# Attention over a key and value cache, one token: key-value groups taken in pairs

## The chip, the cores and the metric

One core of a Trainium2 chip. The metric is the device time of one execution in microseconds. A core has TensorE (PE), VectorE (DVE), ScalarE (ACT), GpSimd (POOL) and SyncE (SP), which here issues all large loads from device memory (HBM) into on-chip memory (SBUF, 128 partitions); 16 DMA engines carry them. TensorE adds up in PSUM.

## The reference

One new token (a row of 512) goes through an attention block and an MLP block. The attention has 32 query heads, 8 key-value groups of 4 query heads each, a cache of 16384 tokens a group and 128 values a token; all tensors are bf16.

```python
q = (layernorm(x) @ wq).reshape(1, 1, 32, 128)           # wq: 512 x 4096, 4 MB
scores = einsum(q, k) * 128 ** -0.5                      # k_cache: 8 groups x 16384 x 128, 32 MB
o = einsum(softmax(scores), v)                           # v_cache: the same size, 32 MB
h = x + o.reshape(1, 1, 4096) @ wo                       # wo: 4096 x 512, 4 MB
# block B on layernorm(h), S = 1: its four shifted quarters take other tokens, of which there
# are none, so they are zero and x1 is its input
x1 = layernorm(h)
out = h + x1 + gelu(layernorm(x1) @ w3) @ w4             # w3: 512 x 1792, w4: 1792 x 512
```

Each byte of the cache and of the weights is used once: 79 MB are read and 1 KB is written.

## The kernel before

The kernel records operations by engine (class `Program`), with what each reads and writes; `emit` puts them out engine by engine in recorded order and derives the semaphore waits. Nothing is rescheduled, so each engine, SP too, works through its list in order, and one that waits holds back all that stands behind it.

**Buffers.** Four buffers of 32 KB a partition (`rb`, 4 MB each) form a ring. The list `ORDER` deals the large loads out to them in turn: query weights, keys 0, keys 1, then values g and keys g+2 for each group g, at last the output weights and the MLP weights. A load waits until the last reader of its buffer is done: for keys the DVE transpositions, for values the products with them, for the query weights the query products. A fifth buffer of the same size, `kt`, holds the transposed keys in eight slices.

**Queries.** Layer norm on 128 partitions (`row_sums`, `variance`, `seeds`, `inverse_root`) gives `xn`. 128 products (L363) with one moving column make the 32 query heads as columns `QT`; four selecting products (L369) and four copies (L374) spread them into `qb`, in which zeros stand around each query so that a shifted window picks the output rows.

**One group** (loop over g from 0 to 8, in which the values of group g-1 stand between the steps of group g):
- `transpose_keys`: eight DVE transpositions (L384), each of 1024 32-bit words a partition (pairs of bf16), from `rb` to `kt`.
- `scores`: 32 products (L392) of 512 columns into one PSUM bank. 128 output rows are 32 parts of the tokens times 4 heads, 512 columns are the tokens of a part.
- `max_a` (L399) takes the maximum of a row, `max_b` (L403, L405) turns the 128 maxima into a row and takes one for each head, `max_c` (L409, L411) spreads them back as the bias, and ACT makes Exp and its sum (L414). `weights` transposes the result into `pt` (L419), `denominator` adds the sums up (L423).
- `values`: 32 products (L433), four side by side in column groups of the array: 16 stationary columns (4 token rows x 4 heads) against 512 moving columns (4 token rows x 128). Only the blocks in which both token rows agree are wanted.
- `gather`: a copy of the whole bank to SBUF (L441) and four fp32 products (L444) with the selecting matrix `zo`, which pick the wanted blocks and add them up in `A_ps` over all groups.
- then SP gets the loads of values g and keys g+2 (all loads are at L216).

**The end.** `A_ps` is normalised (L487 to L493) to `o_b`; 128 products with the output weights (L499); layer norm; 16 products with w3 (L514); Gelu (L527); transpositions (L531); 56 products with w4 (L538); the sum (L542); the store (L544). `spin` puts idle products on PE in between (L245). The output weights are loaded in two pieces and the MLP weights in six, so that products can begin before all has landed.

Of the kernel before, what the change touches and what calls it, by code (L numbers as in the profile page):

```python
# [109 lines left out]
D = 512  # L110
HQ = 32
# [11 lines left out]
RING = 4  # L123
ORDER = [("wq", 0), ("k", 0), ("k", 1)]
ORDER += [x for g in range(HKV) for x in (("v", g), ("k", g + 2)) if x[1] < HKV] + [("wo", 0), ("ffn", 0)]
SLOT = {x: n % RING for n, x in enumerate(ORDER)}
QB, PB, FB = SLOT["wq", 0], SLOT["wo", 0], SLOT["ffn", 0]
# [7 lines left out]
def bass_sequential_preLN__gqa_block_cached__mixer_s_mlp__decode_kernel(  # L135
# [13 lines left out]
    with ExitStack() as ctx:  # L149
# [12 lines left out]

        x4 = sb("x4", [4, 128], BF16)
# [3 lines left out]
        selq_f = sb("selq_f", [128, 4, 32], FP32)  # L167
        quarter = sb("quarter", [4, 4, 32], BF16)
        selq = sb("selq", [128, 4, 4, 32], BF16)
        row32 = sb("row32", [128, 32], FP32)  # L170
        maskdd = sb("maskdd", [128, 4], FP32)
        zo = sb("zo", [128, 4, 240], FP32)
        zd = sb("zd", [128, 240], FP32)
# [5 lines left out]
        QT = sb("QT", [128, HQ], BF16)  # L179
        qb = sb("qb", [128, 4, HKV, QW], BF16)  # L180
        mx = sb("mx", [128, 1], FP32)
        nm = sb("nm", [128, REP], FP32)
        nmh = sb("nmh", [128, REP], FP32)
        bias = sb("bias", [128, 1], FP32)
        acc = [sb(f"acc{i}", [128, 1], FP32) for i in range(2)]
        p_sb = sb("p_sb", [128, 512], BF16)
        pt = [sb(f"pt{i}", [128, 16, 32], BF16) for i in range(2)]
        o_sb = [sb(f"o_sb{i}", [128, 512], FP32) for i in range(2)]
# [13 lines left out]
        rb = [sb(f"rb{i}", [128, 128 * DH], BF16) for i in range(RING)]  # L202
        kt = sb("kt", [128, 128 * DH], BF16)
        wq_sb, wo_sb = rb[QB], rb[PB]
        w3_sb = rb[FB][:, 0:NCH * FM].rearrange("p (k f) -> p k f", k=NCH)
        w4_sb = rb[FB][:, NCH * FM:2 * NCH * FM].rearrange("p (m c) -> p m c", m=NHC)
# [11 lines left out]
        def load_whole(i, src):  # L218
            load(f"r{i}", rb[i][:, :], src, ("r", i, 0), also=[("r", i, n) for n in range(1, RPARTS)])

        def load_tokens(kind, g):

            src = A_k_cache if kind == "k" else A_v_cache
            load_whole(SLOT[kind, g], src[0, g].rearrange("(p t) d -> p (t d)", p=128))
# [17 lines left out]
        def spin(n):  # L242

            for _ in range(n):
                pe(lambda e: e.matmul(O_ps[1][:, :], pt[0][:, 0:4, :].rearrange("p n u -> p (n u)"), p_sb[:, :],  # L245
                                      start=True, stop=True), r=["p", ("pt", 0)], w=[("O", 1)], bank=[("O", 1)])
# [61 lines left out]
        load_whole(QB, A_wq.rearrange("(p k) c -> p (k c)", k=NCH))  # L308
        load_tokens("k", 0)
        load_tokens("k", 1)  # L310
# [3 lines left out]
        dve(lambda e: e.memset(selq_f[:, :, :], 0.0), w=["selq_f"])  # L314
# [3 lines left out]
        for b in range(2):  # L318
            for e_ in range(2):
                n = 2 * b + e_  # L320
                P.op("POOL", lambda e, n=n, b=b, e_=e_: e.affine_select(
                    out=selq_f[:, n, :], in_=selq_f[:, n, :], pattern=[[-2, 32]], compare_op=ALU.not_equal,
                    fill=1.0, base=-(64 * b + e_), channel_multiplier=1), r=["selq_f"], w=["selq_f"])
# [16 lines left out]
        dve(lambda e: e.tensor_copy(selq[:, :, :, :], selq_f[:, :, :].unsqueeze(2).to_broadcast([128, 4, 4, 32])),  # L340
            r=["selq_f"], w=["selq"])
        dve(lambda e: e.memset(nscale[:, :], -SCALE), w=["nscale"])
        act(lambda e: e.activation(scr[0:1, 0:1], mean4[0:1, 0:1], ACTF.Exp), r=["mean4"], w=["scr"])
        for i in range(2):
            dve(lambda e, i=i: e.memset(O_ps[i][:, :], 0.0), w=[("O", i)], bank=[("O", i)])
        dve(lambda e: e.memset(zo[:, :, :], 0.0), w=["zo"])
        dve(lambda e: e.memset(zd[:, :], 0.0), w=["zd"])
        pool(lambda e: e.memset(qb[:, :, :, :], 0.0), w=["qb"])  # L348
        dve(lambda e: e.tensor_reduce(row32[:, :], ident_f[:, :].rearrange("p (c r) -> p r c", c=4), AX.X, ALU.add),
# [3 lines left out]
        dve(lambda e: e.tensor_copy(  # L353
            zo[:, :, 112:128].rearrange("p j (h d) -> p j h d", d=4),
            row32[:, 0:16].rearrange("p (j h) -> p j h", j=4).unsqueeze(3).to_broadcast([128, 4, 4, 4])),
            r=["row32"], w=["zo"])
        dve(lambda e: e.tensor_copy(zd[:, 112:128].rearrange("p (h d) -> p h d", d=4),
                                    maskdd[:, :].unsqueeze(2).to_broadcast([128, 4, 4])), r=["maskdd"], w=["zd"])


        for h in range(HQ):
            for k in range(NCH):
                pe(lambda e, h=h, k=k: e.matmul(n_ps[:, h:h + 1],  # L363
                                                wq_sb[:, k * HQ * DH + h * DH:k * HQ * DH + (h + 1) * DH],
                                                xn[:, k:k + 1], start=(k == 0), stop=(k == NCH - 1)),
                   r=["xn", ("r", QB, 0)], w=["n"], bank=["mn"])
        dve(lambda e: e.tensor_copy(QT[:, :], n_ps[:, 0:HQ]), r=["n"], w=["QT"], bank=["mn"])
        for n in range(4):
            pe(lambda e, n=n: e.matmul(m_ps[:, n * HQ:(n + 1) * HQ],  # L369
                                       selq[:, n, :, :].rearrange("p a i -> p (a i)"), QT[:, :],  # L370
                                       start=True, stop=True), r=["selq", "QT"], w=["m"], bank=["mn"])
        for a in range(4):
            lo, hi, at = 32 * a, 32 * a + 32, QPAD + 32 * a
            dve(lambda e, lo=lo, hi=hi, at=at: e.tensor_copy(  # L374
                qb[lo:hi, :, :, at:at + REP].rearrange("p n g h -> p (n g) h"),
                m_ps[lo:hi, 0:4 * HQ].rearrange("p (n h) -> p n h", h=REP)), r=["m"], w=["qb"], bank=["mn"])


        def transpose_keys(g, ts):
            i = SLOT["k", g]  # L380
            for t in ts:
                view = lambda x, t=t: x[:, :].bitcast(I32).rearrange("p (x l w) -> p x (l w)", x=2, l=64)[
                    :, :, t * 512:(t + 1) * 512]
                dve(lambda e, i=i, view=view: e.transpose(view(kt), view(rb[i])),  # L384
                    r=[("r", i, n) for n in range(RPARTS)], w=[("kt", t)])
# [3 lines left out]
        def scores(g, cs):  # L389
            for c in cs:  # L390
                for n in range(4):
                    pe(lambda e, g=g, n=n, c=c: e.matmul(  # L392
                        s_ps[:, g % 2, :], qb[:, n, g, QPAD - 4 * c:QW - 4 * c],
                        ktv[:, n // 2, n % 2, :, 8 * c:8 * c + 8, :],
                        start=(c == 0 and n == 0), stop=(c == 7 and n == 3)),
                       r=["qb", ("kt", c)], w=[("s", g % 2)], bank=[("s", g % 2)])

        def max_a(g):
            dve(lambda e, g=g: e.tensor_reduce(mx[:, :], s_ps[:, g % 2, :], AX.X, ALU.max),  # L399
                r=[("s", g % 2)], w=["mx"], bank=[("s", g % 2)])  # L400

        def max_b():
            pe(lambda e: e.matmul(m_ps[0:1, 0:128], mx[:, :], ident_f[:, :], start=True, stop=True),  # L403
               r=["mx", "ident_f"], w=["m"], bank=["mn"])
            dve(lambda e: e.tensor_reduce(nm[0:1, :], m_ps[0:1, 0:128].rearrange("o (n h) -> o h n", h=REP),  # L405
                                          AX.X, ALU.max), r=["m"], w=["nm"], bank=["mn"])

        def max_c(g):
            pe(lambda e: e.matmul(n_ps[:, 0:REP], nscale[0:1, :], nm[0:1, :], start=True, stop=True),  # L409
               r=["nm", "nscale"], w=["n"], bank=["mn"])  # L410
            dve(lambda e: e.scalar_tensor_tensor(nmh[:, :], n_ps[:, 0:REP], 1.0, maskdd[:, :], ALU.mult, ALU.mult,  # L411
                                                 accum_out=bias[:, :]), r=["n", "maskdd"], w=["nmh", "bias"],
                bank=["mn"])
            act(lambda e, g=g: e.activation(p_sb[:, :], s_ps[:, g % 2, :], ACTF.Exp, bias=bias[:, 0:1],  # L414
                                            scale=float(SCALE), accum_out=acc[g % 2][:, :]),
                r=[("s", g % 2), "bias"], w=["p", ("acc", g % 2)], bank=[("s", g % 2)])

        def weights(g):
            dve(lambda e, g=g: e.transpose(pt[g % 2][:, :, :].rearrange("p n u -> p (n u)"), p_sb[:, :]),  # L419
                r=["p"], w=[("pt", g % 2)])  # L420

        def denominator(g):
            pe(lambda e, g=g: e.matmul(A_ps[:, 128:129], zd[:, 112 - 16 * g:240 - 16 * g], acc[g % 2][:, :],  # L423
                                       start=(g == 0), stop=(g == HKV - 1), skip_group_check=True),
               r=[("acc", g % 2), "zd"], w=["A"], bank=["A"])

        def values(g, qs):
            i = SLOT["v", g]
# [20 lines left out]
        for g in range(HKV + 1):  # L449
# [4 lines left out]
            if g:  # L454
                values(g - 1, range(2))
# [122 lines left out]
```

## Time and profile before

| | |
|---|---|
| median of 3 runs | 192.53 us (192.48 to 192.58) |
| the profiled execution | 192.57 us, span 191.0 us |
| granted TensorE clock, mean | 0.865 |
| busy: PE, DVE, ACT, POOL | 125.0, 107.5, 10.1, 8.9 us |
| load queue of SP | 79.17 MB, 97.1% of 16 DMA engines over the span |
| loads on that queue | 25: 17 of 4096 KB, 8 smaller |

The span runs from the first to the last instruction of the core; the time of an execution is 1.57 us longer. A line like `L384 DVE STREAM_TRANSPOSE kt<-rb` gives source line, engine, operation and what it writes and reads. In the timeline, the first column is the start in us and the second how long the row's instructions took together; a bracket at the end gives the idle time of the engine before it and what ended it. The packet records of the trace list, for each piece that a DMA engine moves, its queue, start, duration and size; here a piece is one partition's row of a load.

### The profile page before, as it was taken

The page shows a single profiled execution, that of the slowest core. Times are in us where ns is not written, and L with a number is a line of the kernel's source. Part 1 is how long each engine was busy: PE and PEld are TensorE (multiplying, and loading weights), DVE is VectorE, ACT ScalarE, POOL GpSimd, SP SyncE. Part 2 cuts the span into 40 slices and gives each one's busy share as a digit, 9 for nine tenths or more (in the row PEclk, how much of TensorE's full clock was granted, in tenths as well). Part 3 has the DMA queues.
Part 4 walks back from the last instruction along what each step waited for, and adds up shares of the span by engine and source line. Part 5 has one row for each costly group of instructions (what it writes and reads, how often), then busy time and mean ns, then how long its engine had stood idle before and what let it go on. Part 6 is the DMA issues. An engine that isn't in the chain of part 4 may idle for free.

```text
span 191.0 us, 2257 instructions
## 1 busy us (share of the span) xinstructions
PE 125.0 (65%) x979; PEld 56.4 (30%) x979; DVE 107.5 (56%) x178; ACT 10.1 (5%) x22; POOL 8.9 (5%) x19
## 2 busy tenths in 40 slices
PE   1025079579889825993499539972996199736894
PEld 1025024224332321432133313340333033312632
DVE  5822099399399317932794259435953495303171
ACT  3000000100100100010000100010001000400010
POOL 6400000000000000000000000000000000000042
PEclk9999999859999995899569975995798569988699
DMA  6999999999999999999999999999999999999991
GB/s 227 432 439 436 439 439 434 439 439 432 425 422 419 419 425 432 432 429 439 439 439 439 429 425 432 425 425 419 439 419 436 425 439 439 439 396 407 419 399 74
DMA packets 3624, 79.29 MB, mean 415 GB/s; under 512 B 416, under 2 KB 544, under 8 KB 1056
## 3 DMA queue, kind: packets, MB, share of 16 engines
q1 hardware_dynamic: 3608, 79.17, 97.1%
q8 instruction: 7, 0.11, 0.2%
q14 instruction: 1, 0.01, 0.0%
q10 hardware_dynamic: 8, 0.00, 0.0%
HBM read 79.17 MB, written 0.00 MB: 414 GB/s over the span
## 4 chain that ended last, share of the span: by engine, by line
DMA 70%; DVE 21%; PE 6%; SPq 1%; issue 1%; ACT 0%; ACTq 0%
DMA rb<-in_A_k_cache_dram 56%; DVE kt L384 20%; DMA rb<-in_B_w_dram 14%; PE s_ps L392 5%; SPq L216 1%; ACT p_sb L414 0%; DVE pt L419 0%; DVE mx L399 0%; PE mn_ps L538 0%; PE mn_ps L409 0%; PE mn_ps L403 0%; DVE nm L405 0%; DVE fin L542 0%; DVE nmh L411 0%; SPq L101 0%
## 5 line engine op out<-in xcount | busy, mean ns | idle before, releaser
L392 PE MATMUL s_ps<-kt,qb 128*128 128x512 bf16 x256 | 74.1, 452 | 32.8 <-DVE kt L384 32.2
L384 DVE STREAM_TRANSPOSE kt<-rb 128x1024 int32<-128x1024 int32 x64 | 73.0, 1209 | 28.3 <-DMA rb<-in_A_k_cache_dram 28.3
L392 PEld LDWEIGHTS s_ps<-kt,qb 128*128 128x128 bf16 x256 | 27.0, 111 | 77.4 <-DVE kt L384 41.1
L433 PE MATMUL O_ps<-rb,pt 128*16 128x512 bf16 x256 | 20.6, 410 | 3.2 <-DMA rb<-in_A_v_cache_dram 3.2
L444 PE MATMUL A_ps<-o_sb,zo 128*128 128x128 f32 x64 | 9.7, 297 | 7.4 <-DVE o_sb L441 7.4
L414 ACT ACTIVATE p_sb<-s_ps,bias 128x512 bf16<-128x512 f32 x8 | 5.5, 688 | 155.3 <-DVE nmh L411 155.3
L399 DVE TENSOR_REDUCE mx<-s_ps 128x1 f32<-128x512 f32 x8 | 5.5, 692 | 12.4 <-PE s_ps L392 12.4
L444 PEld LDWEIGHTS A_ps<-o_sb,zo 128*128 128x128 f32 x64 | 8.1, 198 | 8.9 <-DVE o_sb L441 8.9
L419 DVE STREAM_TRANSPOSE pt<-p_sb 128x512 bf16<-128x512 bf16 x8 | 5.7, 711 | 7.3 <-ACT p_sb L414 7.3
L441 DVE COPY o_sb<-O_ps 128x512 f32<-128x512 f32 x8 | 5.3, 657 | 8.0 <-PE O_ps L433 8.0
L363 PE MATMUL mn_ps<-xn,rb 128*128 128x1 bf16 x128 | 3.5, 165 | 9.3 <-DMA rb<-in_A_wq_dram 9.3
L433 PEld LDWEIGHTS O_ps<-rb,pt 128*16 128x16 bf16 x256 | 5.9, 91 | 9.8 <-DMA rb<-in_A_v_cache_dram 4.3
L297 POOL TENSOR_SCALAR st<-st 128x1 f32<-128x1 f32 x1 | 0.3, 265 | 176.0 <-DVE st L282 176.0
L363 PEld LDWEIGHTS mn_ps<-xn,rb 128*128 128x128 bf16 x128 | 3.5, 104 | 9.4 <-issue 9.4
L423 PE MATMUL A_ps<-acc,zd 128*128 128x1 f32 x16 | 3.3, 273 | 2.3 <-ACT p_sb L414 2.3
L403 PE MATMUL mn_ps<-ident_f,mx 128*1 128x128 f32 x16 | 3.0, 271 | 2.5 <-DVE mx L399 2.5
L499 PE MATMUL O_ps<-rb,o_b 128*32 128x128 bf16 x128 | 3.4, 300 | 1.8 <-DMA rb<-in_A_wo_dram 1.8
L245 PE MATMUL O_ps<-p_sb,pt 128*128 128x512 bf16 x17 | 4.5, 381 | 0.0
L405 DVE TENSOR_REDUCE nm<-mn_ps 1x4 f32<-1x128 f32 x8 | 2.2, 278 | 3.8 <-PE mn_ps L403 3.8
L423 PEld LDWEIGHTS A_ps<-acc,zd 128*128 128x128 f32 x16 | 2.6, 203 | 5.9 <-ACT p_sb L414 5.9
L348 POOL MEMSET qb<- 128x4992 bf16 x1 | 4.3, 4258 | 0.0
L499 PEld LDWEIGHTS O_ps<-rb,o_b 128*32 128x32 bf16 x128 | 3.2, 142 | 1.9 <-DVE o_b L493 1.9
(74 smaller groups left out, 42.7 us busy)
## 6 DMA issues: line engine op xcount, KB each, us to landing
rb<-in_A_k_cache_dram SPq DMA_DIRECT2D x8, 4096.0 KB, 29.8
rb<-in_A_v_cache_dram SPq DMA_DIRECT2D x8, 4096.0 KB, 34.5
rb<-in_A_wq_dram SPq DMA_DIRECT2D x1, 4096.0 KB, 12.2
rb<-in_A_wo_dram SPq DMA_DIRECT2D x1, 3072.0 KB, 33.0
rb<-in_B_w_dram SPq DMA_DIRECT2D x1, 1344.0 KB, 23.3
rb<-in_A_wo_dram SPq DMA_DIRECT2D x1, 1024.0 KB, 35.1
rb<-in_B_w_dram SPq DMA_DIRECT2D x1, 768.0 KB, 25.5
rb<-in_B_w_dram SPq DMA_DIRECT2D x1, 512.0 KB, 26.3
```

Of the source, the lines that this page charges most:

```text
L245: pe(lambda e: e.matmul(O_ps[1][:, :], pt[0][:, 0:4, :].rearrange("p n u -> p (n u)"), p_sb[:, :], start=True, stop=True), r=["p", ("pt", ...
L363: pe(lambda e, h=h, k=k: e.matmul(n_ps[:, h:h + 1], wq_sb[:, k * HQ * DH + h * DH:k * HQ * DH + (h + 1) * DH], xn[:, k:k + 1], start=(k == ...
L384: dve(lambda e, i=i, view=view: e.transpose(view(kt), view(rb[i])), r=[("r", i, n) for n in range(RPARTS)], w=[("kt", t)])
L392: pe(lambda e, g=g, n=n, c=c: e.matmul(s_ps[:, g % 2, :], qb[:, n, g, QPAD - 4 * c:QW - 4 * c], ktv[:, n // 2, n % 2, :, 8 * c:8 * c + 8, ...
L399: dve(lambda e, g=g: e.tensor_reduce(mx[:, :], s_ps[:, g % 2, :], AX.X, ALU.max), r=[("s", g % 2)], w=["mx"], bank=[("s", g % 2)])
L414: act(lambda e, g=g: e.activation(p_sb[:, :], s_ps[:, g % 2, :], ACTF.Exp, bias=bias[:, 0:1], scale=float(SCALE), accum_out=acc[g % 2][:, :]),
L419: dve(lambda e, g=g: e.transpose(pt[g % 2][:, :, :].rearrange("p n u -> p (n u)"), p_sb[:, :]), r=["p"], w=[("pt", g % 2)])
L423: pe(lambda e, g=g: e.matmul(A_ps[:, 128:129], zd[:, 112 - 16 * g:240 - 16 * g], acc[g % 2][:, :], start=(g == 0), stop=(g == HKV - 1), sk ...
L433: pe(lambda e, q=q, ct=ct, xl=xl, ch=ch: e.matmul(O_ps[g % 2][32 * ct:32 * ct + 16, :], pt[g % 2][:, xl, 4 * ch:4 * ch + 16], tiles[:, xl ...
L441: dve(lambda e, g=g: e.tensor_copy(o_sb[g % 2][:, :], O_ps[g % 2][:, :]), r=[("O", g % 2)], w=[("osb", g % 2)], bank=[("O", g % 2)])
L444: pe(lambda e, g=g, j=j: e.matmul(A_ps[:, 0:128], zo[:, j, 112 - 16 * g:240 - 16 * g], o_sb[g % 2][:, j * 128:(j + 1) * 128], start=False, ...
L499: pe(lambda e, r_=r_, q=q: e.matmul(O_ps[0][32 * q:32 * q + 32, 0:128], copies(o_b[:, r_:r_ + 1], 32), wo_sb[:, r_ * D + q * 128:r_ * D + ...
```

## The change

Two groups are worked on at once: partitions 0 to 63 hold the first group's tokens and 64 to 127 the second's, each partition 256 tokens (64 KB of keys and 64 KB of values).

- **Buffers and loads.** The ring goes. `vb` (64 KB a partition) takes the values of a pair as one load of 8 MB with rows of 64 KB; `kb[0]` and `kb[1]` (32 KB) take the keys of a pair as two loads, the first and the second half of each row. The values of the last pair come as two loads (rows of 48 and 16 KB). The query weights lie in `vb`, the output weights in `kb[0]`, the MLP weights in `kb[1]`. The order is query weights, keys of pair 0 (two halves), values 0, keys of pair 1, values 1, and so on, then the weights as before. The next keys wait for the transpositions from their own buffer, the next values for all products with the values before.
- **Queries.** 32 products with 512 moving columns, `xn` repeated over 64 stationary columns, put the heads of a pair as rows into four PSUM banks; eight DVE transpositions (`qcol`) and four copies make `qb`. The selecting matrices and their five preparing steps, the 128 narrow products, `QT` and two PSUM clears go.
- **Softmax.** One for a pair: maximum and Exp run over 1024 columns in two banks, with 8 heads in the bias. The weights are transposed in two steps of 64 partitions into `pt`, which is zeroed once and holds the two groups in columns of their own. One `pt`, one `acc`. Values stand after the softmax of their own pair, no longer between the steps of the next group.
- **Values.** 64 products a pair, as before two groups had, with 32 stationary columns instead of 16.
- **Gather.** Instead of copy and four products: four DVE steps multiply each block of 128 columns of the bank with a 0/1 mask of rows (`rowc`) and add them up in `od`; one fp32 product with `zo` puts the sum into `A_ps`.

The diff, cut to its core:

```diff
-RING = 4
-ORDER = [("wq", 0), ("k", 0), ("k", 1)]
-ORDER += [x for g in range(HKV) for x in (("v", g), ("k", g + 2)) if x[1] < HKV] + [("wo", 0), ("ffn", 0)]
+PAIRS = HKV // 2
+V3 = ((0, 3), (3, 4))
...
-        rb = [sb(f"rb{i}", [128, 128 * DH], BF16) for i in range(RING)]
+        kb = [sb(f"kb{i}", [128, 128 * DH], BF16) for i in range(2)]
+        vb = sb("vb", [128, 256 * DH], BF16)
         kt = sb("kt", [128, 128 * DH], BF16)
...
+        def pair_rows(src, j):
+            return src[0, 2 * j:2 * j + 2].rearrange("g (u t) d -> (g u) (t d)", u=64)
+
+        def load_keys(j, y):
+            n = 128 * DH
+            load(f"k{y}", kb[y][:, :], pair_rows(A_k_cache, j)[:, y * n:(y + 1) * n], ("r", y, 0),
+                 also=[("r", y, i) for i in range(1, RPARTS)])
+
+        def load_values(j):
+            src = pair_rows(A_v_cache, j)
+            if j < PAIRS - 1:
+                load("v", vb[:, :], src, ("v", 0), also=[("v", 1)])
+            else:
+                n = 64 * DH
+                for i, (lo, hi) in enumerate(V3):
+                    load(f"v3{i}", vb[:, lo * n:hi * n], src[:, lo * n:hi * n], ("v", i))
...
+        rows = [(O_ps[0][:, :], ("O", 0)), (O_ps[1][:, :], ("O", 1)), (s_ps[:, 0, :], ("s", 0)), (s_ps[:, 1, :], ("s", 1))]
+        for j, (row, key) in enumerate(rows):
             for k in range(NCH):
+                for g in range(2):
+                    at = k * HQ * DH + (2 * j + g) * REP * DH
+                    pe(lambda e, row=row, k=k, g=g, at=at: e.matmul(
+                        row[64 * g:64 * g + 64, :], copies(xn[:, k:k + 1], 64), wq_sb[:, at:at + REP * DH],
+                        start=(k == 0), stop=(k == NCH - 1)), r=["xn", ("v", 0)], w=[key], bank=[key])
+            for b in range(2):
+                dve(lambda e, j=j, b=b, row=row: e.transpose(
+                    qcol[:, j, 2 * REP * b:2 * REP * (b + 1), :].rearrange("p m u -> p (m u)"),
+                    row.rearrange("p (h b i e) -> p b e h i", b=2, i=32, e=2)[:, b, :, :, :]),
+                    r=[key], w=["qcol"], bank=[key])
...
+        def softmax(j):
+            s_all = s_ps[:, :, :].rearrange("p y f -> p (y f)")
+            dve(lambda e: e.tensor_reduce(mx[:, :], s_all, AX.X, ALU.max), r=[("s", 0), ("s", 1)], w=["mx"], **both)
...
+            act(lambda e: e.activation(p_sb[:, :], s_all, ACTF.Exp, bias=bias[:, 0:1], scale=float(SCALE),
+                                       accum_out=acc[:, :]),
+                r=[("s", 0), ("s", 1), "bias"], w=["p", "acc"], **both)
+            for g in range(2):
+                dve(lambda e, g=g: e.transpose(pt[64 * g:64 * g + 64, :, :, g, :], p_sb[64 * g:64 * g + 64, :]),
+                    r=["p"], w=["pt"])
...
+        def values(j):
+            tiles = vb[:, :].rearrange("p (x c l d) -> p x l c d", x=4, c=8, l=8)
+            for q in range(16):
                 for ct in range(4):
+                    xl, ch = 2 * q + ct // 2, ct % 2
+                    parts = [int(xl // 8 >= V3[1][0])] if j == PAIRS - 1 else [0, 1]
                     pe(lambda e, q=q, ct=ct, xl=xl, ch=ch: e.matmul(
+                        O_ps[j % 2][32 * ct:32 * ct + 32, :], pt[:, xl, ch, :, :].rearrange("p g u -> p (g u)"),
+                        tiles[:, xl // 8, xl % 8, 4 * ch:4 * ch + 4, :], start=(q == 0), stop=(q == 15)),
+                       r=[("v", n) for n in parts] + ["pt"], w=[("O", j % 2)], bank=[("O", j % 2)])
+
+        def gather(j):
+            O, key = O_ps[j % 2], ("O", j % 2)
+            for c in range(4):
+                block = O[:, c * 128:(c + 1) * 128]
+                if c == 0:
+                    dve(lambda e, block=block: e.tensor_scalar(od[:, :], block, rowc[:, 0:1], None, ALU.mult),
+                        r=[key, "rowc"], w=["od"], bank=[key])
+                else:
+                    dve(lambda e, block=block, c=c: e.scalar_tensor_tensor(
+                        od[:, :], block, rowc[:, c:c + 1], od[:, :], ALU.mult, ALU.add),
+                        r=[key, "rowc", "od"], w=["od"], bank=[key])
+            pe(lambda e: e.matmul(A_ps[:, 0:128], zo[:, 96 - 32 * j:224 - 32 * j], od[:, :], start=False,
+                                  stop=(j == PAIRS - 1), skip_group_check=True),
+               r=["od", "zo"], w=["A"], bank=["A"])
+
+        load_values(0)
+        for j in range(PAIRS):
+            for y in range(2):
+                transpose_keys(y, range(8))
+                scores(j, y, range(8))
+                if j < PAIRS - 1:
+                    load_keys(j + 1, y)
+            softmax(j)
+            values(j)
+            gather(j)
+            if j < PAIRS - 1:
+                load_values(j + 1)
```

## The prediction

> **What bounds the kernel now.** I read the page first, then the chain in order of time, the timeline of SP's issues, the timeline of the last 27 us, and the packet records of the trace.
>
> The page, sections 1 to 3 (queue lines: packets, MB, share of 16 engines' time):
>
> ```profile
> span 191.0 us, 2257 instructions
> PE 125.0 (65%) x979; PEld 56.4 (30%) x979; DVE 107.5 (56%) x178; ACT 10.1 (5%) x22; POOL 8.9 (5%) x19
> ...
> DMA  6999999999999999999999999999999999999991
> GB/s 227 432 439 436 439 439 434 439 439 432 425 422 419 419 425 432 432 429 439 439 439 439 429 425 432 425 425 419 439 419 436 425 439 439 439 396 407 419 399 74
> ...
> q1 hardware_dynamic: 3608, 79.17, 97.1%
> q8 instruction: 7, 0.11, 0.2%
> ```
>
> No compute engine is over 65%; the load queue is full from the second slice to the last but one. 97.1% of 191.0 us is 185.5 us of transfer that can't be overlapped with itself. The change moves the same bytes, so only three things can move the time: the cost of moving them, a hole in the stream, and the work behind its end.
>
> The chain that ended last, in order of time (start us, us, what):
>
> ```profile
> 121.07 29.50 DMA rb<-in_A_k_cache_dram
> 150.57 0.02 issue
> 150.60 9.14 DVE kt L384 x8
> 159.77 0.03 issue
> ...
> 161.59 26.81 DMA rb<-in_B_w_dram
> 188.40 0.04 issue
> 188.45 0.57 PE mn_ps L538 x16
> 189.02 0.02 issue
> 189.04 0.29 DVE fin L542
> ```
>
> The 20% of DVE in this chain is no limit: the weights issued at 159.8 us, after the last key transposition, wait behind loads that are already queued and land in order. The real end is the last weight piece at 188.40 us; 2.6 us follow it (0.57 product, 0.29 sum, the store and its landing).
>
> SP's issues, in the timeline (start us, us, instruction):
>
> ```profile
> 16.72 0.33 SPq L216 DMA_DIRECT2D rb<-in_A_k_cache_dram  x1
> 33.19 0.33 SPq L216 DMA_DIRECT2D rb<-in_A_v_cache_dram  x1
> 47.66 0.33 SPq L216 DMA_DIRECT2D rb<-in_A_k_cache_dram  x1
> ```
>
> Keys 0 land at 23.97 us (the chain's first transfer ends there), keys 7 at 150.57: thirteen 4 MB loads later, so 9.74 us a load. Each issue comes two or three loads ahead of its turn, and the queue never empties.
>
> **The stream, costed.** In the packet records a row of 32,768 B takes 1216 ns (median of 2176), 24,576 B 915 ns, 8192 B 313 ns. The slope is 0.0367 ns a byte, with 12 ns a packet left over. Value rows of 64 KB in pairs 0 to 2 replace 48 packets on each of the 16 DMA engines by 24, so 24 x 12 ns = 0.29 us is saved. Packets overlap by some 3.5 ns, which makes 0.2 us the lower estimate. If a 64 KB row is still moved as two packets, the saving is nothing. No row shows such a packet; as the fit is straight from 8 to 32 KB I take 0.24. Pair 3's values (48 and 16 KB rows) keep their packet count. Three loads fewer save three completion packets of 9 ns, 0.03 us. Sum: -0.27 us, bounds -0.32 and 0.
>
> Keys become halves of 64 KB rows: still 32 KB a packet, only the pitch in memory doubles. The trace has reads of part of a row: the output weights (24 KB and 8 KB out of 32 KB) run at the fitted line, and so do the MLP weights with 14 KB pitch (10,752 B in 407 ns). I cost it at nothing. The Trainium skill speaks against it here ("DMA: Bandwidth & Descriptors", Latency and other measured facts): copies slow down when the row pitch is a large power of two, from 207 of 214 GB/s at 512 KiB to 103 at 4 MiB. Its smallest pitch is eight times this one; an estimate by its 3% over the 67 MB of keys and values would be +5 us. No run here shows it.
>
> **Holes.** The ring gives way to one value buffer of 64 KB and two key buffers, so each issue has a new condition, and SP waits in program order: a late one holds back all behind it. With 9.74 us a unit, in the new order: first half of keys of pair 0 at 23.97, second 33.7, values 53.2, keys of pair 1 at 62.9 and 72.7, and from there 38.9 us a pair. Worst cases:
> - Values 0 wait for the 32 query products. The query weights are in at 13.04. Products of 512 columns took 0.43 us each at half clock (scores from 25.29 on); all serial that is 13.7 us, so issue by 26.7, needed by 33.7.
> - Keys of pair 1, first half, wait for the first 8 transpositions. DVE first has 8 query transpositions of 256 columns (0.57 each by the 224-column row, mostly beside the products) and four copies of 0.29: free by 29; then 9.14: issue at 38, needed by 53.2. Second half: 48 against 62.9.
> - Values 1 wait for values 0 to be read: softmax done by 57, then 64 products. The last group's 32 took 3.50 us cold, 109 ns each (16 warm took 1.04): 7.0 us, issue at 64, needed by 72.7. This is the thinnest margin, 8.7 us, and it repeats in each pair.
> - Output weights wait for transpositions over at 150, MLP weights for 159.8; their turn is 170.
>
> So no hole, price 0. If the cover goes, each us past 8.7 costs one.
>
> **The tail.** What the one softmax for a pair lengthens shows only after the last keys. These are the rows of before:
>
> ```profile
> 161.34 0.69 DVE L399 TENSOR_REDUCE mx<-s_ps 128x1 f32<-128x512 f32 x1 [1.62 <-PE s_ps L392]
> ...
> 164.33 0.71 DVE L419 STREAM_TRANSPOSE pt<-p_sb 128x512 bf16<-128x512 bf16 x1 [0.91 <-ACT p_sb L414]
> ...
> 170.06 3.50 PE L433 MATMUL O_ps<-rb,pt 128*16 128x512 bf16 x32 [3.22 <-DMA rb<-in_A_v_cache_dram]
> ...
> 177.48 3.36 PE L499 MATMUL O_ps<-rb,o_b 128*32 128x128 bf16 x128 [1.82 <-DMA rb<-in_A_wo_dram]
> ```
>
> Keys still land at 150.57 (fifteenth unit in both orders). From mx to the end of pt took 3.70 us. The maximum doubles its columns (+0.54, 0 to 0.69), Exp too (+0.5, 0 to 0.69), and the weight transposition becomes two of 1024 columns on 64 partitions: by columns 2 x 1.4 = 2.8, by elements 1.4; I take 2.8, so +2.1. pt is ready at 168.2, not 165.0. Then 64 products instead of 32, three quarters of them with values landed at 165.2: 4.2 us warm, 7.0 cold, ending at 172.4 to 175.2 (before: 173.56). The diagonal sums replace a copy (0.69) and 8 products (1.16) by four DVE steps on 128 columns (0.29 to 0.35 each, 1.4) and two passes (0.38): a wash. Normalising follows as before 1.98 and 1.17 us later: o_b at 175.5 to 178.3 against 176.71. It is needed when the first output-weight piece lands (177.48), and behind that the MLP's last products wait 0.29 and 0.30 us for their weights: 0.59 more is free. Cost 0 to 0.2; I take 0.
>
> The query products (128 to 32), the fewer gathers and the removed set-up lie under the loads and count nothing: queries are needed at 23.97, end at the latest at 29, and the 5 us is taken up before the values of pair 0 arrive.
>
> **Sum.** The profiled execution took 192.57 us (191.0 span, 1.57 around it), the median of the runs is 192.53. 192.57 - 0.27 = 192.30; from the median 192.26. I predict 192.3. About 0.2%, 0.39 us, is what a measurement can tell from no change: 192.14 and 192.92 are the limits.
>
> **Rivals.**
> 1. *The last DMA engine ends earlier: faster, 191.9.* The 1 KB packets of the last piece fall in two groups: eight engines are through at 186.1 to 186.7 us, eight at 187.4 to 188.26. There are eight instruction packets inside the span (seven of 16 KB on q8, one of 8 KB on q14), and beside a q8 packet an engine stood still for 1.0 us and its next row took 0.48 longer. So one fetch costs one engine 1.5 us, and the slowest such engine sets the end. PE's instructions fall from 979 to 799 pairs, so some fetches go, but at least five stay; a gain comes only if the latest engine (0.24 behind the next) is spared, or the packets save their full 0.29: 192.57 - 0.32 - 0.3 = 191.95. Against: who is hit can't be read from a page. Chance 0.33. The Trainium skill ("Runtime: NRT & Kernel Launch", Instruction fetch mechanics) has these 16 KiB blocks of 256 instructions and calls their cost mostly hidden; by that nothing is gained here, and the trace disagrees, with 1.5 us on the engine that is hit.
> 2. *The tail becomes compute: slower, up to 194.9.* pt is written in runs of 16 elements at 64 partitions. If that doubles the transpositions (5.7 us) and PE has gone cold, the products end at 178.1, o_b comes at 181.2 and the output product starts 3.7 late: less 0.59, +3.1 at worst; with one of the two, about +0.2 to +0.5. It decides once o_b passes 178.1. For: PE idles some 6 us before these products, and it ran at half speed after 3.2 us idle in the line at 170.06. Chance 0.12.
> 3. *Doubled pitch or long rows slow the stream: slower, 194 to 195.* At 425 GB/s, a common slice of the page, instead of 431 (16 x 32,768 B in 1216 ns), 67 MB take 2.2 us more. Against: full rows and part rows run alike. Chance 0.06. A hole in the queue: 0.01.
> 4. *The rows are split, nothing is saved:* 192.5, within my forecast's class.
>
> Forecast 0.48 (192.15 to 192.9). Faster 0.33, same 0.48, slower 0.19. Range 191.7 to 193.2: rival 1 whole, and the cheaper half of rival 2.
>
> **What would show it.** Right: the DMA row full, V packets of 65,536 B near 2420 ns, last piece at about 188.1 us, o_b before 178. A 0 or low digit inside the DMA row means a hole; 64 KB packets well over 2432 ns mean rival 3; the output product starting on DVE o_b after 178, with the last weights already in, means rival 2; an earlier last landing with equal packets means rival 1.

## The result, and the profile after

| | before | changed |
|---|---|---|
| median of the runs beside each other | 192.58 us (192.48 to 192.78, 9 runs) | 192.09 us (191.84 to 192.36, 9 runs) |
| profiled execution, its span, the rest | 192.57, 191.04, 1.53 | 192.01, 190.70, 1.31 |
| last weight piece landed | 188.40 | 188.06 |

The ratio is 0.9973 [0.9962, 0.9983], so the kernel is faster by a quarter of a per cent. The forecast was 192.3 in the class of no measurable change. The time lies in the range, 0.21 below the forecast and 0.05 past the limit to "faster" (192.14). All ratios here are of runs in the chip's usual state; only e3 below has runs in a slower one, three of its six (207.36 to 208.01 us), its profile among them.

The page of the changed kernel, sections 1 to 3 (busy time and share; DMA load in 40 slices; queues with packets, MB and share):

```profile
span 190.7 us, 1877 instructions
PE 117.2 (61%) x797; PEld 45.6 (24%) x799; DVE 114.8 (60%) x176; ACT 8.7 (5%) x14; POOL 7.7 (4%) x16
...
DMA  6999999999999999998999999979999998999991
...
q1 hardware_dynamic: 3176, 79.17, 97.1%
q8 instruction: 6, 0.10, 0.2%
```

The same bytes go in 432 packets less: 24 rows and three completion packets on each of 16 engines. The digits of 7 and 8 inside the row are no holes. In the packet records, cut at the ends of the slices, the 16 engines are busy for all of each slice from the second to the last but one (1.00 to 1.02 of the time), the three with low digits (from 85.8, 124.0 and 157.3 us) too. The chain of the changed kernel in order of time (start us, us, what) ends in the same three steps as before:

```profile
120.53 29.58 DMA kb<-in_A_k_cache_dram
150.10 0.02 issue
150.12 9.14 DVE kt L393 x8
...
161.12 26.94 DMA kb<-in_B_w_dram
188.06 0.04 issue
188.10 0.59 PE mn_ps L535 x16
188.70 0.02 issue
188.72 0.29 DVE fin L539
```

The work behind the last landing takes 2.64 us in both (188.40 to 191.04, 188.06 to 190.70), so the span's whole gain, 0.34, comes from the stream. This figure rests on one profile of each. Two further ones (e9 and e11 below) have the last landing at 188.22 and 188.06, and over all runs the mean span is 191.08 us before and 190.74 (here) or 190.80 (e9) after, a gain of 0.28 to 0.34. SP's issues in the timeline of the changed kernel:

```profile
18.78 0.33 SPq L218 DMA_DIRECT2D vb<-in_A_v_cache_dram  x1
31.78 10.81 SPq L218 DMA_DIRECT2D kb<-in_A_k_cache_dram  x2
59.30 0.33 SPq L218 DMA_DIRECT2D vb<-in_A_v_cache_dram  x1
```

The keys of pair 1 are issued at 31.8 and 42.3 and the values of pair 1 at 59.3, all ahead of their turns (53.2, 62.9 and 72.7). Last, the compute tail in the timeline of the changed kernel:

```profile
160.39 1.23 DVE L412 TENSOR_REDUCE mx<-s_ps 128x1 f32<-128x1024 f32 x1 [1.14 <-PE s_ps L401]
...
164.35 2.49 DVE L427 STREAM_TRANSPOSE pt<-p_sb 64x1024 bf16<-64x1024 bf16 x2 [1.33 <-ACT p_sb L423]
...
166.99 5.49 PE L439 MATMUL O_ps<-vb,pt 128*32 128x512 bf16 x64 [2.04 <-DVE pt L427]
...
177.00 2.23 PE L496 MATMUL O_ps<-kb,o_b 128*32 128x128 bf16 x96 [2.26 <-DMA kb<-in_A_wo_dram]
```

The brackets tell who is late. The value products now wait for the softmax (before, for the last values), but the output products still wait for their weights, not for `o_b` (ready at 175.79).

### The profile page after: what moved, and what is told of

It is laid out like the page before. It is cut to its first block, busy times and chain, and to the rows that moved or that the text cites. A ratio compares the mean times of both kernels' runs of the same rounds, so it can differ in the third digit from the quotient of the medians.

```text
span 190.7 us, 1877 instructions
## 1 busy us (share of the span) xinstructions
PE 117.2 (61%) x797; PEld 45.6 (24%) x799; DVE 114.8 (60%) x176; ACT 8.7 (5%) x14; POOL 7.7 (4%) x16
## 4 chain that ended last, share of the span: by engine, by line
DMA 77%; DVE 19%; SPq 1%; issue 0%; PE 0%
DMA kb<-in_A_k_cache_dram 63%; DVE kt L393 19%; DMA kb<-in_B_w_dram 14%; SPq L218 1%; PE mn_ps L535 0%; DVE fin L539 0%; SPq L101 0%
## 5 line engine op out<-in xcount | busy, mean ns | idle before, releaser
L401 PE MATMUL s_ps<-kt,qb 128*128 128x512 bf16 x256 | 70.0, 416 | 19.1 <-DVE kt L393 16.6
L393 DVE STREAM_TRANSPOSE kt<-kb 128x1024 int32<-128x1024 int32 x64 | 73.0, 1210 | 11.6 <-DMA kb<-in_A_k_cache_dram 11.6
L401 PEld LDWEIGHTS s_ps<-kt,qb 128*128 128x128 bf16 x256 | 23.3, 104 | 64.8 <-DVE kt L393 38.8
L439 PE MATMUL O_ps<-vb,pt 128*32 128x512 bf16 x256 | 23.6, 550 | 16.8 <-DMA vb<-in_A_v_cache_dram 14.7
L439 PEld LDWEIGHTS O_ps<-vb,pt 128*32 128x32 bf16 x256 | 8.9, 132 | 29.9 <-DMA vb<-in_A_v_cache_dram 15.0
L427 DVE STREAM_TRANSPOSE pt<-p_sb 64x1024 bf16<-64x1024 bf16 x8 | 9.9, 1239 | 5.4 <-ACT p_sb L423 5.3
L423 ACT ACTIVATE p_sb<-s_ps,bias 128x1024 bf16<-128x1024 f32 x4 | 4.5, 1114 | 156.7 <-DVE nmh L419 156.7
L412 DVE TENSOR_REDUCE mx<-s_ps 128x1 f32<-128x1024 f32 x4 | 4.9, 1225 | 4.5 <-PE s_ps L401 4.5
L453 DVE SCALAR_TENSOR_TENSOR od<-O_ps,rowc,od 128x128 f32<-128x128 f32 x12 | 4.2, 351 | 0.4
L331 DVE CAST ident<-ident_f 4x4 bf16<-4x4 f32 x1 | 3.8, 3849 | 0.6 <-POOL ident_f L326 0.6
## 6 DMA issues: line engine op xcount, KB each, us to landing
vb<-in_A_v_cache_dram SPq DMA_DIRECT2D x1, 2048.0 KB, 31.8
```

The source lines that it names most:

```text
L331: dve(lambda e: e.tensor_copy(ident[:, :], ident_f[0:4, 0:4]), r=["ident_f"], w=["ident"])
L393: dve(lambda e, view=view: e.transpose(view(kt), view(kb[y])), r=[("r", y, n) for n in range(RPARTS)], w=[("kt", t)])
L401: pe(lambda e, n=n, c=c: e.matmul(s_ps[:, y, :], qb[:, n, j, QPAD - 4 * c:QW - 4 * c], ktv[:, n // 2, n % 2, :, 8 * c:8 * c + 8, :], start ...
L412: dve(lambda e: e.tensor_reduce(mx[:, :], s_all, AX.X, ALU.max), r=[("s", 0), ("s", 1)], w=["mx"], **both)
L423: act(lambda e: e.activation(p_sb[:, :], s_all, ACTF.Exp, bias=bias[:, 0:1], scale=float(SCALE), accum_out=acc[:, :]), r=[("s", 0), ("s", ...
L427: dve(lambda e, g=g: e.transpose(pt[64 * g:64 * g + 64, :, :, g, :], p_sb[64 * g:64 * g + 64, :]), r=["p"], w=["pt"])
```

## The experiments

Three theories went on record. **A**, rows: the stream's end is its bytes plus some 11 to 12 ns a packet on each DMA engine, and all else is hidden. **F**, fetches: the end is set by the DMA engine that instruction packets hit last (rival 1). **T**, tail: where `o_b` comes late, compute sets the end (rival 2). The kernel before ran beside them, at 192.61 to 192.65 us. The diffs are against the changed kernel and cut to their core.

### e1_v32 and e2_v16: values in shorter rows

```diff
-                load("v", vb[:, :], src, ("v", 0), also=[("v", 1)])
+                n = 256 * DH // VK                                   # VK = 2 (e1), 4 (e2)
+                for i in range(VK):
+                    load(f"v{i}", vb[:, i * n:(i + 1) * n], src[:, i * n:(i + 1) * n], ("v", i))
```

> The changed kernel, with the values of pairs 0 to 2 loaded as two loads each (column halves, rows of 32 KB) instead of one with rows of 64 KB; nothing else differs. Theory A (rows): each of the 16 DMA engines again carries 24 more rows at 11 to 12 ns each and 3 more completion packets: +0.30 us over the changed kernel, 192.4, last weight piece 0.3 us later. Rival F (instruction fetches): the instructions are the same, so the fetches are: +0.0, 192.1. The packet medians should read 1216 ns for 32 KB.

> As the run with halves, but with four loads for each pair's values (rows of 16 KB). Theory A: 72 rows more on each engine than with 64 KB rows, 72 x 11.5 ns = 0.83, and 9 more completion packets, 0.08: +0.9 us, 193.0, and the step from halves to quarters is twice the step from one to halves. Rival F: +0.0, 192.1.

e1 took 192.39 us, ratio to before 0.9988 [0.9979, 0.9996]; e2 192.82, ratio 1.0009 [1.0001, 1.0018]. The chain's end, first of e1, then of e2:

```profile
161.24 27.18 DMA kb<-in_B_w_dram
188.42 0.04 issue
```

```profile
161.94 26.77 DMA kb<-in_B_w_dram
188.72 0.04 issue
```

The last landing moves 188.06, 188.42, 188.72. e1 costs 0.30 us for 24 more rows an engine, e2 0.43 more for 48: 12.5 and 9 ns a row, the completion packets of the added loads counted in. The mean spans (190.74 to 190.80 for the changed kernel, 191.00, 191.51) part more evenly: 0.20 to 0.26, then 0.51, so 8 to 11 ns a row. A holds and asked a little too much of e2 (193.0); F's 192.1 falls for both.

e1 tells apart more than the rows. It has the packet count of the kernel before (3608 on the queue) and lands its last byte where that did (188.42 against 188.40), so the rest of the change, the tail and the fetches among it, gives the stream next to nothing (one profile each; the mean spans differ by 0.08). What e1 still gains on the kernel before, 0.22 us, lies for the most part outside the span: the mean of the runs' spans is 191.00 against 191.08, that of the time around them 1.38 against 1.55.

### e9_after and e11_kball: the changed kernel again, and its key buffers as one tensor

```diff
-        kb = [sb(f"kb{i}", [128, 128 * DH], BF16) for i in range(2)]
+        kb_all = sb("kb", [128, 256 * DH], BF16)
+        kb = [kb_all[:, i * 128 * DH:(i + 1) * 128 * DH] for i in range(2)]
```

> The changed kernel once more, on one chip with the two others of this call. 192.1 us, span 190.7, 1.33 us around the span.

> The changed kernel with kb[0] and kb[1] as the two halves of one tensor; loads, rows, instructions and their order are the same. It asks for the time around the span, which was 1.31 to 1.38 us in the changed kernel and in six variants of it, but 1.64 and 1.68 in the two that had such a tensor (they also loaded keys whole), and 1.55 in the kernel before. If the place of the buffers is the cause: 1.65 around the span and 192.4. If it is the whole load of the first keys, or anything else: 1.33 and 192.1.

e9 took 192.10 us, ratio 0.9975 [0.9965, 0.9984], so the result repeats. e11 took 192.12, ratio 0.9975 [0.9966, 0.9984]. The question behind e11 was the time around the span, the execution's time less its span. Its mean is 1.33 us for the changed kernel (9 runs), 1.35 in e9, 1.38 in e11 as in e1; in the two kernels with whole key loads below, e4 and e7, it is 1.64 and 1.68. How the key buffers lie is not the cause, nor is the number of instructions (1.31 with 4979 of them, in e3). What is stays open; e4 and e7 also share the whole load of pair 0's keys, which no run tried alone and which the kernel before does not have.

### e5_fill10 and e3_fill18: more instruction fetches

Idle products of one column, into an unused corner of PSUM, make PE's program longer (`fill`): 642 of them in e5, 1550 in e3.

```diff
+        def fill(n):
+            for _ in range(n):
+                pe(lambda e: e.matmul(m_ps[0:4, 200:201], ident[:, :], x4[:, 0:1], start=True, stop=True),
+                   r=["ident", "x4"], w=["fill"], bank=["mn"])
...
+        fill(300)          # before the query products, in both
+                fill(3)    # behind each slice of scores; e3: 5
+                fill(50)   # behind each gather but the last; e3: 180, and 130 before the values
```

> The changed kernel with fewer tiny idle products than in the run with 1550, spread so that PE should never run behind: 300 before the query products, 3 after each slice of the scores, 50 after the gather of pairs 0 to 2. 1284 more PE instructions, so 10 fetches of 16 KB while loads run, instead of 5. Theory F8 (from the run with 1550, where 17 fetches left 8 engines late by 3 us, one by 1 us and 7 not at all): the fetches go round 8 of the 16 engines, so up to 8 cost nothing more than one does, and the ninth and tenth hit two engines again: last weight piece 1.5 us later, 193.6 us. Rival (fetches spread over all 16 engines, or cost nothing): 192.1.

> The changed kernel with 1550 tiny idle products on PE (4 rows x 1 column, about 28 ns with their weight load), put where PE waits anyway: 300 before the query products, 5 after each slice of the scores, 130 before the values and 180 after the gather of pairs 0 to 2. Some 3100 more PE instructions, 12 more fetches of 16 KB, about 17 or 18 in the stream with the one of 8 KB. The loads are unchanged. Theory A: only rows and bytes count, +0.0, 192.1; every delay of PE stays under the cover of 8.7 us. Rival F: with more fetches than DMA engines at least one engine is hit twice and ends 1.5 us later: 193.6. A third reading, that the time outside the span goes with the number of instructions (it is 1.53 us before and 1.31 after), would show there: +1.9 us for 3100 more by 0.22 for 360.

e5 took 193.42 us (193.38 to 193.60), ratio 1.0040 [1.0027, 1.0054]: 1.3 us more than the changed kernel, with the same loads and the same packets. Its page and its chain:

```profile
q1 hardware_dynamic: 3176, 79.17, 96.4%
q8 instruction: 11, 0.18, 0.4%
```

```profile
161.29 28.23 DMA kb<-in_B_w_dram
189.51 0.04 issue
```

In the packet records, PE's fetches of 16 KB come about once in 256 of its instructions. Each stops one DMA engine for 1.0 to 1.1 us, and the next row there often takes 0.46 to 0.55 us longer. By the 1 KB packets of the last piece, the engines of e5 end in three groups: seven at 185.8 to 186.5, seven at 187.1 to 187.6, and two at 189.25 and 189.42. Ten fetches lie inside the stream, and one of 8 KB that another engine has; the ninth and the tenth hit two engines that had been hit already, and these two carry the end. The seven engines that were never hit end as early as in the changed kernel (185.8 to 186.3 there), so no hole has come in. So F's mechanism is real, with its price of about 1.5 us: each kernel here whose loads end last ends with an engine that was hit, in the changed kernel at 187.92, where those never hit were through by 186.3. But it parts two kernels only once an engine is hit twice, in e5 by the ninth fetch. The changed kernel has five fetches inside the stream, the one before seven, and each has the 8 KB one besides: six engines are late in one and eight in the other, but in both the latest was hit once. This is why some 180 fewer products on PE gained nothing in the stream.

The Trainium skill ("Runtime: NRT & Kernel Launch", Instruction fetch mechanics) calls the cost of a fetch mostly hidden. For the engine that waits for its instructions e5 agrees but for one stretch, 2.7 us among the 300 idle products at the start; for a kernel that ends with its loads, e5's 1.3 us says otherwise.

e3 was meant for the second round of fetches, and missed every expectation: 205.17 us over all six runs (200.29 to 208.01), ratio 1.0488 [1.0440, 1.0536] by the three lower ones. The loads did land at 189.5, eight engines of them hit twice (189.1 to 189.5), seven not at all (186.0 to 186.3). So fetches go round eight of the sixteen engines. But the chain no longer runs through the loads. PE in the timeline of e3, of its longest run:

```profile
148.34 3.91 PE L262 MATMUL mn_ps<-x,ident 4*4 4x1 bf16 x151
155.68 0.86 PE L262 MATMUL mn_ps<-x,ident 4*4 4x1 bf16 x29 [3.42 <-issue]
156.47 1.89 PE L407 MATMUL s_ps<-kt,qb 128*128 128x512 bf16 x4
```

Between two idle products, from 152.25 us, PE stands for 3.42 us and waits for nothing that the profile shows; a fetch starts 1.1 us into this in the packet records (153.4). That products of 26 ns use up their instructions faster than they come, because the fetch waits behind long rows on its engine, is argued, not shown. Behind the stop PE ran at half clock (0.50 granted from 157 to 160 us), and a slice of scores with its five products took 2.0 us there, more than the 1.2 of the transposition that feeds it. e3 shows a second price of dense small products, and settles nothing on the change.

### e6_late: a hole in the queue

The next pair's keys are issued only when the values of this pair have been read.

```diff
-                if j < PAIRS - 1:
-                    load_keys(j + 1, y)
             softmax(j)
             values(j)
+            if j < PAIRS - 1:
+                for y in range(2):
+                    load_keys(j + 1, y, after=[("O", j % 2)])
```

> The changed kernel, but both loads of the next pair's keys are issued only when the values of the pair have been read; buffers, rows and instructions are the same. Theory: only the lead of the issues keeps the stream full. Now the queue runs empty three times, from the landing of a pair's values until its 64 products are done and one issue later: 5.4 to 6.2 us of products and 1.0 us from issue to first packet, so 6.5 to 7.2 us each, +20 us: 212, with three low digits in the DMA row. Rival (the order of loads does not matter, the engines' work is hidden either way): 192.1.

It took 220.38 us, ratio 1.1438 [1.1406, 1.1470], 8 us worse than expected. The DMA row of its page shows what the prediction had named as the sign of a hole:

```profile
DMA  7898998990299999890399999880599999899992
```

```profile
53.02 5.77 PE O_ps L439 x59
...
59.67 41.53 DMA vb<-in_A_v_cache_dram
...
101.23 5.56 PE O_ps L439 x35
```

In the chain above the loads wait for the value products in every pair. The period is 48.0 us (issues of keys at 58.81 and 106.81), not 38.9: some 5.6 us of products, and 3.5 us where 1.0 had been put down for the restart. The packet records show where most of it goes. Before the second hole fifteen engines were through with the values at 99.0 to 99.5 us, the sixteenth at 100.9; the products began at 101.2, and the next keys' first rows came at 107.8 to 108.8, 1.0 to 2.0 us after their issue. So an engine stood idle for 8.7 us on average: a load can be used only when its slowest engine is through, and the lag of that one (some 1.4 us; one instruction fetch, at 89.3, fell into this stretch) is paid at every hole. The last 0.4 us are open.

### e4_kwhole: keys too in rows of 64 KB

Pairs 0 and 2 get both halves of their keys as one load into one buffer.

```diff
+        def load_keys_whole(j):
+            keys = [("r", y, i) for y in range(2) for i in range(RPARTS)]
+            load("kw", kb_all[:, :], pair_rows(A_k_cache, j), keys[0], also=keys[1:])
```

> The changed kernel with the keys of pairs 0 and 2 as one load of 64 KB rows (pairs 1 and 3 stay halves, so that each load's buffer is still free in time). Theory A: 16 rows and 2 completion packets less on each engine: -0.2 us, 191.9. Pair 0's keys land 10 us later, at 33, under the cover. Rival F: +0.0, 192.1. If the whole load of pair 2 is issued too late (its buffer is free 9 us after the second half of pair 1 has landed, its turn comes 19 us after), a hole in the stream would show as a low digit in the DMA row and more than 192.1.

Expected faster, it was slower: 193.93 us, ratio 1.0043 [1.0016, 1.0070]. Of its runs five lie at 192.2 to 192.7 and seven at 193.9 to 194.8. The stream seems to have gained: its last packet ended at 187.76 us, 0.16 before that of the changed kernel (187.92; 188.10 in e9, 187.87 in e11). But the keys of pair 2 land whole at 111.3, so 16 transpositions start there at once, and the lateness runs on into pair 3. The tail in the timeline of e4:

```profile
163.30 1.23 DVE L416 TENSOR_REDUCE mx<-s_ps 128x1 f32<-128x1024 f32 x1 [1.14 <-PE s_ps L405]
...
179.33 3.60 PE L502 MATMUL O_ps<-kb,o_b 128*32 128x128 bf16 x128 [1.10 <-DVE o_b L496]
```

The maximum comes 2.9 us later than in the changed kernel, and the output products now wait for `o_b` with all weights there. That is T, as the prediction had described its sign. No profile shows one of the five shorter runs; e8 and e10 below suggest why they lost nothing. A row of 64 KB is worth some 10 ns; the time until its first half can be used costs 9.7 us of lead.

### e8_v3whole and e10_v3whole: the last values in rows of 64 KB

```diff
-V3 = ((0, 3), (3, 4))
+V3 = ((0, 4),)
```

> The changed kernel with the values of the last pair as one load of 64 KB rows instead of 48 and 16 KB: 8 rows less on each engine, but the 64 products of the last pair start when all has landed, at 170 instead of 167.0. Theory T (tail, second rival of the prediction): o_b comes 3 to 4.5 us later, the output products start at 179 to 180.4 instead of 177.0; 0.6 to 0.7 us of that is free, the rest is paid: 193.3 to 194.7 us. Rival A (only the stream counts): -0.1, 192.0.

> The kernel with the last pair's values as one load once more, beside the changed kernel on the same chip. By the rows (theory A) 8 rows and one completion packet less on each engine: 0.1 us faster than the changed kernel; by the first run of it 0.2. If the tail binds after all (output products starting at 178.3 with PE cold), up to 1.5 us slower.

The same kernel twice: in e8 191.86 us, ratio 0.9961 [0.9948, 0.9975], by four runs; in e10 192.77, ratio 1.0010 [0.9984, 1.0037], by twelve, six at 191.83 to 192.12 and six at 193.43 to 193.91. The timeline of e8 (191.83), then of e10's profiled run (193.91):

```profile
169.55 5.39 PE L439 MATMUL O_ps<-vb,pt 128*32 128x512 bf16 x64 [4.56 <-DMA vb<-in_A_v_cache_dram]
...
178.31 1.97 PE L496 MATMUL O_ps<-kb,o_b 128*32 128x128 bf16 x128 [1.11 <-DVE o_b L490]
```

```profile
169.79 6.25 PE L439 MATMUL O_ps<-vb,pt 128*32 128x512 bf16 x64 [4.75 <-DMA vb<-in_A_v_cache_dram]
...
179.42 3.60 PE L496 MATMUL O_ps<-kb,o_b 128*32 128x128 bf16 x128 [1.11 <-DVE o_b L490]
```

In both the products wait for `o_b`. In e8 the 128 products take 1.97 us and end at 180.28, no later than in the changed kernel (180.45), so the end stays with the loads. In e10 they take 3.60 and end at 183.02, and the last sum starts at 190.60 instead of 188.72. The two lengths of the same products are PE at full and at half clock: the granted clock is 1.00 in e8 while they run and 0.50 in e10. Of the 2.7 us between the two ends, 1.6 lie in these products and 1.1 in `o_b` (178.25 and 179.36), which came later mostly because the value products, too, ran longer (5.39 and 6.25 us, clock 0.67 and 0.57). So between these two runs T is decided by the clock that PE has in the last 20 us. The twelve runs of e10 agree: the six short ones have a mean clock of 0.836 to 0.847, the six long ones 0.813 to 0.823. What decides the clock from run to run was not tried. The changed kernel's split of the last values (48 and 16 KB) lets the value products begin at 166.99 instead of 169.6, and none of its 18 runs here is above 192.45, though five have a clock as low as e10's long ones (0.818 to 0.821).

### e7_best: the rows of pair 0's keys and fewer weight pieces

Pair 0's keys as one load, w3 as one load instead of two, w4 in three pieces (6, 7 and 1 rows) instead of four.

```diff
-W3 = ((0, 3), (3, 4))
-W4 = ((0, 6), (6, 10), (10, 13), (13, 14))
+W3 = ((0, 4),)
+W4 = ((0, 6), (6, 13), (13, 14))
```

> The changed kernel with fewer, longer rows where the tail allows: the keys of pair 0 as one load of 64 KB rows, w3 as one load instead of two, w4 as three pieces (6, 7 and 1 rows) instead of four. 24 rows and 3 completion packets less on each engine. Theory A: 24 x 9 to 11 ns, -0.25 us, 191.85. The keys of pairs 1 to 3 stay halves, so DVE has caught up with the late first pair by pair 1 or 2. Against it: all 16 w3 products wait for the landing of the whole w3, which may take 0.3 of the 0.6 to 0.7 us that the tail has to spare; if more, 192.1 or above.

It took 192.71 us, ratio 1.0003 [0.9994, 1.0012], no gain over the kernel before. The end of its chain:

```profile
187.81 0.57 PE mn_ps L539 x28
188.39 0.32 PE O_ps L261
188.71 0.20 PE mn_ps L539 x4
```

The last packet ended at 187.65 us, 0.27 earlier than in the changed kernel, as costed, but 28 products wait for the larger piece (landed at 187.77), and behind them stand an idle product (0.32, L261) and the last four. The last sum starts at 188.93, later than the 188.72 of the changed kernel; the time around the span (1.68) adds 0.35. No version tried beats the changed kernel in all its runs.

## Why the prediction was right, and where it was not

- **The bound** was read rightly: both chains end in the last weight piece with the same 2.64 us behind it, and no compute engine of the changed kernel is over 61%.
- **The rows.** Predicted 24 rows x 12 ns less some overlap, 0.24. In the packet records a row of 65,536 B takes 2421 ns (predicted near 2420), two of 32,768 B 2432: 24 x 11 ns = 0.26, or 0.19 with the 3 ns by which packets overlap; by e1 0.20 to 0.30. That the rows are split (rival 4) is out. With the three completion packets this makes 0.22 to 0.29 of the profiled 0.34. In that execution the first packets also started some 0.1 us earlier on average than in the profile before (1.92 and 2.03), which is chance: in e9, the same kernel, they start at 2.07.
- **The doubled pitch** costs nothing: key packets of 32,768 B take 1216 ns in both kernels, so rival 3 is out. The Trainium skill's rule on row pitch ("DMA: Bandwidth & Descriptors", Latency and other measured facts), which the prediction had stretched far below its smallest pitch to +5 us, does not show in this kernel at 64 KB.
- **No hole.** Every issue came before the worst case of the text (values 0 at 18.8 for 26.7, keys of pair 1 at 31.8 and 42.3 for 38 and 48, values 1 at 59.3 for 64). The one stated sign failed: digits of 7 and 8 in the DMA row, where the packet records have all engines at work. e6 shows what a hole looks like, 0 and 2, and that "each us past 8.7 costs one" was too cheap.
- **The tail** cost nothing, as said, though its steps were off in part. The maximum started at 160.39, 0.95 earlier than before, where the text had no shift, and the two transpositions took 1.25 each, not 1.4, so `pt` was ready at 166.8, not 168.2; maximum and Exp were near their costs. The value products took 5.49, between the 4.2 and 7.0 of the text, and `o_b` came at 175.8, at the lower bound (175.5 to 178.3).
- **Rival 2** is real, in e4 and e10. Its stated point, `o_b` after 178.1, was incomplete: in e8 `o_b` came at 178.25 and cost nothing. Warm products of 1.97 us give 1.6 us more room than cold ones of 3.60, and the 0.59 us of slack was reckoned from cold ones (3.36).
- **Rival 1** had a time as near as the forecast's (191.9 against 192.3, measured 192.09) and the wrong cause. Both groups of DMA engines moved by some 0.34 (the latest from 188.26 to 187.92). Two engines were spared (six late ones for eight), but the end still went by one that had been hit once. Before, the latest stood 0.15 us behind the next by its packets, not 0.24 as the text read. And e1, with as many fetch packets as the changed kernel, ends where the kernel before did. e5 shows the mechanism with ten fetches.
- **The step that failed** is one that the sum took over unchanged, without a reason: the time around the span. The text carried it as 1.57 us; it is 1.31 in the profiled execution after and 1.53 before. That is 0.22 us, about as much as the rows. The sum by what was measured: 192.57 - 0.34 - 0.22 = 192.01. With the span alone (192.23) the forecast of no measurable change would have been met. Over all runs it is 1.33 after and 1.55 before. So close to half of the gain in time has no known cause; e11 excludes one reason.

## What to carry to other kernels

Where a kernel ends with its loads, cost it as bytes plus a price for each row on each DMA engine, and lengthen rows only where nothing waits for their first part: the last group's values and keys and the last weights should stay in pieces. For each load put the issue beside its turn, since an empty queue costs more than the wait that emptied it (9.1 us for 5.6 in e6); and reckon slack on PE at half clock, as six of e10's twelve runs had it. A difference under 0.3 us can lie outside the span altogether, so compare the span as well as the time.

## What the runs showed of the hardware that was not expected

**Instruction fetches meet eight of sixteen DMA engines in turn**, so the seven of the kernel before and the five of the changed one leave its latest engine equally late, and ten cost 1.3 us more (e5). That eight would still cost nothing more follows from the turn and was not run.

**A small DVE operation stood behind POOL.** At the start of the changed kernel, in the timeline:

```profile
1.70 3.85 DVE L331 CAST ident<-ident_f 4x4 bf16<-4x4 f32 x1 [0.57 <-POOL ident_f L326]
```

```profile
1.60 2.18 POOL L349 MEMSET qb<- 128x2496 bf16 x1
3.72 1.80 POOL L350 MEMSET pt<- 128x2048 bf16 x1
```

A cast of 4 x 4 values, 0.16 us in the kernel before, took 3.85 and ended with the second of two POOL memsets, as in every variant here. The one on `pt` is new. That the cast waited for POOL is read from these ends alone; in the kernel before, the step that makes `xn` took 0.53 us instead of 0.29 and ended with the memset of `qb`, at 7.1. `xn` is ready at 10.5 us instead of 7.1, still ahead of the query weights, so it costs nothing here.

**The time around the span has levels**: 1.31 to 1.38 us in eight kernels, 1.55, 1.64 and 1.68 in three others, within some 0.1 us for each.
